# Transposes of quad 4 dealt into batch 0's scores, and four single PSUM banks as two rings of two

## The chip, the cores and the metric

The kernel runs on one core of one Trainium2 chip. The metric is the device time of one execution in microseconds (us), as the median of several runs. A core has a matrix engine (PE), a vector engine (DVE), a scalar engine for activations (ACT), a general engine (POOL) and a queue engine (SP). Each takes its instructions in the order of its own list; they wait for one another through semaphores. Results of the PE land in PSUM, eight banks of 128 x 512 float32, from which DVE or ACT must read them out before the bank can be written anew.

## The reference

Sigmoid attention over 8 batches of 12 heads, followed by a two-layer network with SiLU:

```python
S = q.shape[2]                                     # q, k, v: (8, 12, 448, 64)
scores = np.matmul(q, k.transpose(0, 1, 3, 2)) / np.sqrt(64) - np.log(S)
attn = 1.0 / (1.0 + np.exp(-scores))
attn_out = np.matmul(attn, v)
x = attn_out.transpose(0, 2, 1, 3).reshape(8 * 448, 768)
h = x @ w_in                                       # w_in: (768, 2048)
g = h * (1.0 / (1.0 + np.exp(-h)))
out = g @ w_out                                    # w_out: (2048, 768)
```

Inputs and output are float32; the kernel computes in float16 with float32 sums.

## The kernel before

**Quads and units.** The work of attention is cut into quads: four heads of one batch, so three quads for a batch and 24 in all. Quad g has seven chunks of keys (ch = 0 to 6), and one chunk of one quad is a unit, numbered n = 7g + ch. For a unit, `scores` issues four 64x64 matmuls (L196) into a pair of PSUM banks (`psc`, two buffers of two banks) and one sigmoid on ACT (L207) that writes `attnT`. `values` multiplies the seven chunks with v (L232, four matmuls for a chunk, 28 for a quad) into two single banks `pav`, one for each half of the rows, and DVE copies them to `xT` (L243). `values(g, end)` with end below 7 does the rounds up to end and keeps the two banks for a later call.

**Transposes.** The scores need k and q with the head's dimension on partitions. For quads 0 to 5 the PE transposes them: `pe_transpose` (L145) takes a list of pieces, and for each takes one single bank (`ptrk` or `ptrq`), issues two matmuls for a chunk against an identity (L153), and has DVE, or ACT for two pieces of quad 0 (L143), copy the bank to `kT` or `qT` (L160). `transposes(g, "k")` is two pieces, chunks 0 to 3 and 4 to 6, so 14 matmuls and two copies; both copies must be done before the quad's scores. Later quads are transposed by DMA.

**The network.** `h_unit(b, fc)` is six matmuls of 128x448 (L262) into a single bank `ph`, then a sigmoid on ACT (`tsig`, L274) and a product on DVE that reads the bank (`gTr`, L276). The second layer's products go to single banks too (`po`, L338). All of this is one generator, `stream`, of which `stretch(ns)` issues a portion.

**Single banks.** Four of the eight PSUM banks are one pool, `ps_1`, with four buffers under one tag. `pw` (dummy matmuls of `keep_busy`), `ptr`, `pav`, `ph`, `po` and some scores (`psc1`) all draw from it. A new tile takes a bank that an earlier tile had, and its first matmul waits for that tile's readers.

**Order of batch 0.** The order is written out by hand. After quad 0's transposes a loop issues `scores` for n = 0 to 23, and behind each what the table `behind` (L554) lists for that n: the rest of quad 0's k, dummy matmuls, transposes of quads 1 to 3, rounds of the values of quads 0 to 2, and the first four matmuls of the first two `h_unit`s (`begin`). Then, for n = 24 to 40 in steps of two, `burst(n, 2)` issues the scores of two units and, if a quad has become complete in an earlier burst, its values; transposes of quads 4 and 5 follow at n = 24, 26, 30 and 32; `stretch` follows each burst. The first `stretch` stands before n = 24: it finishes the two units begun and starts the third.

**Loads.** q, k, v and the weights are loaded by POOL's queue in program order (L82, L113, L120), eight in flight. Further loads are issued when a quad's transposes or values are placed (`after_transpose`, `after_values`).

Of the kernel before, what the change touches and what calls it, by code (L numbers as in the profile page):

```python
# [11 lines left out]
F32 = mybir.dt.float32  # L12
# [5 lines left out]
def kernel(  # L18
# [14 lines left out]
    P = 128  # L33
# [18 lines left out]
    p4 = ctx.enter_context(tc.tile_pool(name="p4", bufs=4))  # L52
    p12 = ctx.enter_context(tc.tile_pool(name="p12", bufs=12))
    ps_sc = ctx.enter_context(tc.tile_pool(name="ps_sc", bufs=2, space=bass.MemoryType.PSUM))
    ps_1 = ctx.enter_context(tc.tile_pool(name="ps_1", bufs=4, space=bass.MemoryType.PSUM))
    ctx.enter_context(tc.manual_schedule())

# [7 lines left out]
    def new_flat(name, g):  # L67
        flat[name, g] = (p3 if name == "v" else p4).tile(
            [P, 2, NCH, D], F16, tag=f"{name}f", name=f"{name}f"
        )  # L70

    def rows_in(name, g):
        b, iq = divmod(g, NQ)
        return source[name][b, 4 * iq : 4 * iq + 4].rearrange(
            "(i h) (p c) d -> (h p) i (c d)", h=2, c=NCH
        )

    def load(names, g, c0=0, c1=NCH):
        for name in names:
            if (name, g) not in flat:  # L80
                new_flat(name, g)
            nc.gpsimd.dma_start(  # L82
                flat[name, g][:, :, c0:c1].rearrange("p i c d -> p i (c d)"),
                rows_in(name, g)[:, :, c0 * D : c1 * D],
            )
# [22 lines left out]
    def load_w_in(step):  # L108
        cols = slice(step * DFF // 4, (step + 1) * DFF // 4)
        rows = moe_w_in[:, cols].rearrange("(iq j h d) f -> h j d iq f", j=2, h=2, d=D)  # L110
        for half in range(2):
            for j in range(2):
                nc.gpsimd.dma_start(  # L113
                    w_in_sb[j * D : (j + 1) * D, half * NQ : (half + 1) * NQ, cols], rows[half, j]
                )
# [13 lines left out]
    def new_qkT(g):  # L129
        for name in ("k", "q"):  # L130
            qkT[name, g] = p4.tile([P, NCH, P], F16, tag=f"{name}T", name=f"{name}T")
# [3 lines left out]
    def keep_busy(n):  # L135
        if n == 0:
            return
        pw = ps_1.tile([P, 512], F32, tag="ps1", name="pw")
        for _ in range(n):
            nc.tensor.matmul(pw, dummy[:, :P], dummy, start=True, stop=True)  # L140

# [3 lines left out]
    def pe_transpose(g, pieces=(("k", 0, 4), ("k", 4, NCH), ("q", 0, 4), ("q", 4, NCH))):  # L145
        if ("k", g) not in qkT:
            new_qkT(g)
        for name, c0, c1, *copy in pieces:
            dst = qkT[name, g].rearrange("p c t -> p (c t)")
            ptr = ps_1.tile([P, 512], F32, tag="ps1", name=f"ptr{name}")  # L150
            for c in range(c0, c1):
                for j in range(2):
                    nc.tensor.matmul(  # L153
                        ptr[j * D : (j + 1) * D, (c - c0) * P : (c - c0 + 1) * P],
                        flat[name, g][:, j, c, :],
                        ident,
                        start=True,
                        stop=True,
                    )
            (copy[0] if copy else nc.vector.tensor_copy)(  # L160
                dst[:, c0 * P : c1 * P], ptr[:, : (c1 - c0) * P]
            )
# [14 lines left out]
    def late_sigmoid():  # L177
        while late:
            to, psc = late.pop()
            nc.scalar.activation(to, psc, AF.Sigmoid, bias=bias_s, scale=QKSCALE)  # L180
# [26 lines left out]
            nc.scalar.activation(to, psc, AF.Sigmoid, bias=bias_s, scale=QKSCALE)  # L207

    def single_banks():
        return [ps_1.tile([P, 512], F32, tag="ps1", name="psc1") for _ in range(2)]  # L210

    xT = {}
    ready = set()
# [4 lines left out]
    def values(g, end=NCH):  # L218
        b, iq = divmod(g, NQ)
        if b not in xT:  # L220
            assert b < 2 or b - 2 in h_done
            xT[b] = p2.tile([P, NPAIR, S], F16, tag="xT", name="xT")
        pav, done_rounds = part_of.pop(g, None) or (
            [ps_1.tile([P, 512], F32, tag="ps1", name="pav") for _ in range(2)],
            0,
        )
        for ch in range(done_rounds, end):
            at = attnT.pop((g, ch))
            for half in range(2):
                own = slice(half * HP, (half + 1) * HP)  # L230
                for j in range(2):
                    nc.tensor.matmul(  # L232
                        pav[half][j * D : (j + 1) * D, :S],
                        flat["v", g][own, j, ch, :],
                        at[own, j, :],
                        start=(ch == 0),
                        stop=(ch == NCH - 1),
                    )
        if end < NCH:
            part_of[g] = pav, end  # L240
            return
        for half in range(2):
            nc.vector.tensor_scalar_mul(xT[b][:, half * NQ + iq, :], pav[half][:, :S], SX)  # L243
        if iq == NQ - 1:
            ready.add(b)
# [9 lines left out]
    def h_unit(b, fc):  # L255
        nonlocal hold, weight
        weight = H_WEIGHT if b > 1 else 1.0
        hold = b > 1 and fc >= NFC - 2 or b == 1 and fc == NFC - 1
        ph = ps_1.tile([P, 512], F32, tag="ps1", name="ph")
        for at, cc in enumerate(pairs):  # L260
            assert b in ready or at < 4
            nc.tensor.matmul(  # L262
                ph[:, :S],
                w_in_sb[:, cc, fc * P : (fc + 1) * P],
                xT[b][:, cc, :],
                start=(at == 0),
                stop=(at == NCC - 1),
            )
            if at < NCC - 1:
                yield 189  # L270
        if fc == NFC - 1:
            h_done.add(b)
        tsig = p3.tile([P, S], F16, tag="tsig", name="tsig")
        nc.scalar.activation(tsig, ph[:, :S], AF.Sigmoid, bias=0.0, scale=ISX)  # L274
        late_sigmoid()
        nc.vector.tensor_mul(  # L276
            gTr[:, fc, (b % 2) * S : (b % 2) * S + S], ph[:, :S], tsig
        )
        yield 189
# [39 lines left out]
    def out_set(a1, rows1, a2, rows2, last=False):  # L319
# [13 lines left out]
        left, right, whole = slice(0, NO2), slice(NO2, DMODEL), slice(0, DMODEL)  # L333

        def product(a, w):
            po = ps_1.tile([P, 512], F32, tag="ps1", name="po")
            for fc in range(NHC):
                nc.tensor.matmul(  # L338
                    po[:, :NO2], a[:, fc, :], w[:, fc, :], start=(fc == 0), stop=(fc == NHC - 1)
                )  # L340
                if fc < NHC - 1:
                    yield 163
            return po[:, :NO2]
# [8 lines left out]
        po = yield from product(a1[:, lo], wq[0][0])  # L352
# [5 lines left out]
        po = yield from product(a1[:, hi], wq[1][0])  # L358
# [5 lines left out]
        po = yield from product(sg[2], tw[3])  # L364
        plus(c22, po, m1)
        yield 163
        po = yield from product(sg[1], tw[2])
# [3 lines left out]
        po = yield from product(a2[:, hi], tw[4])  # L371
        plus(c21, po, c22, -ISX)
        yield 163
        po = yield from product(sg[0], tw[1])
# [4 lines left out]
        po = yield from product(sg[3], wq[1][1])  # L379
# [95 lines left out]
    load("v", 1)  # L475
    load("v", 2)
    load("kq", 3)
    load_w_in(0)

    nc.vector.memset(dummy, 0.5)  # L480
    nc.vector.memset(bias_s, NEG_LOG_S)
# [9 lines left out]
    def after_transpose(g):  # L491
        if g == 0:
            load("kq", 4)
            load_w_in(1)
        elif g == 1:
            load("kq", 5)
        elif g == 4:
            load("kq", 8)
# [24 lines left out]
    def values_if_any():  # L523
        if waiting:
            g = waiting.pop(0)
            values(g)
            after_values(g)

    keep_busy(9)
    pe_transpose(  # L530
        0, (("q", 0, SPLIT), ("k", 0, 1, act_copy), ("q", SPLIT, NCH, act_copy), ("k", 1, FIRST))
# [8 lines left out]
    def transposes(g, name):  # L540
        pe_transpose(g, ((name, 0, 4), (name, 4, NCH)))
        if name == "q":
            after_transpose(g)
# [6 lines left out]
    def begin(fc, steps):  # L550
# [3 lines left out]
    behind = {  # L554
        1: ((rest_of_first_k,),),
        2: ((keep_busy, 2),),
        3: ((transposes, 1, "k"),),
        4: ((transposes, 1, "q"),),
        5: ((keep_busy, 2),),
        6: ((keep_busy, 2),),  # L560
        7: ((keep_busy, 2),),
        8: ((transposes, 2, "k"),),
        9: ((transposes, 2, "q"),),
        10: ((rounds, 0, 2),),
        11: ((rounds, 0, 4),),
        12: ((rounds, 0, 7),),
        13: ((transposes, 3, "k"),),
        14: ((transposes, 3, "q"),),
        15: ((rounds, 1, 2),),
        16: ((rounds, 1, 4),),  # L570
        17: ((rounds, 1, 7),),
        18: ((rounds, 2, 2),),
        19: ((rounds, 2, 4),),
        20: ((rounds, 2, 6),),
        21: ((begin, 0, 4),),
        22: ((rounds, 2, 7),),
# [2 lines left out]
    for n in range(NT_B + 3):  # L579
        scores(*units[n])  # L580
        for do, *what in behind.get(n, ()):
            do(*what)

    TILES = {2: 3, 3: 2, 4: 3, 5: 3, 6: 3, 7: 3}
    paces = {1: 1600, 2: 2400, 3: 2500, 4: 3400, 5: 3200, 6: 3000, 7: 2800}
# [11 lines left out]
    stretch(paces[1])  # L597
    for n in range(NT_B + 3, 2 * NT_B, 2):
        burst(n, 2)
        if n in (24, 30):  # L600
            transposes(4 + (n - 24) // 6, "k")
        elif n in (26, 32):
            transposes(4 + (n - 26) // 6, "q")
        stretch(paces[1])
    values_if_any()
    stretch(21500)
    n = 2 * NT_B
# [39 lines left out]
```

## Time and profile before

| what | us |
|---|---|
| median of three runs | 378.68 (378.37 to 378.78) |
| the profiled execution | 379.04 |
| its span, first to last instruction | 377.3 |
| PE busy in the span | 368.2 |
| ACT busy | 242.9 |
| DVE busy | 234.3 |
| POOL busy | 66.3 |

Starts and lengths in the lines below are in us from the first instruction. In the chain of waits a line is a start, a length and what the chain was on; in the timeline a line is a start, the length of a merged stretch, engine, line of the kernel, operation, what it writes and reads, how many instructions were merged, and in brackets the idle time of the engine before it with what ended it. Matmuls overlap in the PE, so a stretch's length reaches past the start of what follows; the next start tells what the stretch took. A digit in the rows of 40 slices is the busy share of that slice in tenths; one slice is 9.4 us.

### The profile page before, as it was taken

How to read it: one execution, taken by the hardware profiler on the slowest of the kernel's cores; microseconds unless marked ns; L12 is line 12 of the kernel's file. 1: busy time of each engine (PE TensorE's matmuls, PEld its weight loads, DVE VectorE, ACT ScalarE, POOL GpSimd, SP SyncE). 2: the span in 40 equal slices, each digit the busy share in tenths (PEclk: the TensorE clock that was granted, in tenths of full speed). 3: DMA queues.
4: the chain of work that ended last, by engine and by line, in shares of the span. 5: the costliest groups of instructions: out<-in, count | busy, mean ns of one | idle time of the engine just before them, and what ended most of it. 6: DMA issues, size and time to landing. Idle time of an engine off the chain costs nothing.

```text
span 377.3 us, 7624 instructions
## 1 busy us (share of the span) xinstructions
PE 368.2 (98%) x3081; PEld 188.7 (50%) x3081; DVE 234.3 (62%) x417; ACT 242.9 (64%) x355; POOL 66.3 (18%) x99
## 2 busy tenths in 40 slices
PE   7899999999999999999999999999999999999995
PEld 2444445555554455455555545544555445555663
DVE  3456646997666566548577557645676457556773
ACT  5998886778767776676556666667866685243000
POOL 8566423052211103102120200000000000000000
PEclk9999999999999999999999999999999999999999
DMA  8999999989999909919599744546062300110333
GB/s 136 199 204 204 204 204 203 178 126 131 228 208 199 119 2 108 180 42 102 75 162 195 100 111 75 40 118 75 0 138 46 85 2 2 51 33 2 82 86 83
DMA packets 65698, 42.79 MB, mean 113 GB/s; under 512 B 36096, under 2 KB 62208, under 8 KB 65664
## 3 DMA queue, kind: packets, MB, share of 16 engines
q0 software_dynamic: 27072, 22.58, 42.3%
q1 hardware_dynamic: 38240, 19.44, 27.3%
q8 instruction: 24, 0.39, 0.4%
q10 hardware_dynamic: 352, 0.30, 0.2%
q14 instruction: 10, 0.08, 0.1%
HBM read 45.61 MB, written 11.01 MB: 150 GB/s over the span
## 4 chain that ended last, share of the span: by engine, by line
PE 90%; ACT 5%; DMA 2%; issue 1%; POOL 1%; DVE 0%; POOLq 0%; ACTq 0%
PE ph L262 39%; PE po L338 34%; PE psc L196 9%; PE pav L232 8%; ACT attnT L207 4%; DMA qf<-in_q_dram 2%; POOL kf L82 1%; PE ptrq L153 0%; PE ptrk L153 0%; ACT attnT L180 0%; DVE gTr L276 0%; DVE osb L346 0%; ACT kept L412 0%; ACT m L353 0%; ACT tsig L274 0%
## 5 line engine op out<-in xcount | busy, mean ns | idle before, releaser
L207 ACT ACTIVATE attnT<-psc,bias_s 128x896 f16<-128x896 f32 (+1 forms) x168 | 138.2, 896 | 46.1 <-PE psc L196 45.9
L262 PE MATMUL ph<-xT,w_in_sb 128*128 128x448 f16 x768 | 151.2, 353 | 0.0
L276 DVE TENSOR_TENSOR gTr<-ph,tsig 128x448 f16<-128x448 f32 x128 | 78.2, 622 | 69.0 <-ACT tsig L274 68.4
L262 PEld LDWEIGHTS <-w_in_sb 128*128 128x128 f16 x768 | 72.8, 98 | 73.6 <-issue 8.2
L274 ACT ACTIVATE tsig<-ph 128x448 f16<-128x448 f32 x128 | 68.2, 548 | 49.3 <-PE ph L262 48.9
L338 PEld LDWEIGHTS <-S 128*128 128x128 f16 x448 | 42.3, 98 | 33.5 <-issue 6.8
L346 DVE SCALAR_TENSOR_TENSOR osb<-po,osb 128x384 f32<-128x384 f32 x70 | 37.6, 553 | 22.2 <-PE po L338 22.0
L196 PE MATMUL psc<-qT,kT 64*64 64x448 f16 x672 | 48.4, 360 | 1.7 <-ACT qT L143 0.6
L243 DVE TENSOR_SCALAR xT<-pav 128x448 f16<-128x448 f32 x48 | 27.7, 619 | 31.0 <-PE pav L232 31.0
L82 POOL DMA_DIRECT2D vf<-in_v_dram x24 | 17.2, 719 | 163.0 <-PE pav L232 138.8
L338 PE MATMUL po<-T,S 128*128 128x384 f16 x224 | 40.6, 327 | 0.0
L338 PEld LDWEIGHTS <-gTr 128*128 128x128 f16 x304 | 28.7, 98 | 23.5 <-issue 5.4
L338 PE MATMUL po<-w_out_sb,S 128*128 128x384 f16 x224 | 39.9, 326 | 0.0
L232 PE MATMUL pav<-attnT,vf 64*64 64x448 f16 x672 | 38.4, 350 | 0.7 <-DVE gTr L276 0.4
L338 PE MATMUL po<-w_out_sb,gTr 128*128 128x384 f16 x192 | 34.9, 327 | 0.0
L196 PEld LDWEIGHTS <-kT 64*64 64x64 f16 x672 | 16.1, 105 | 29.6 <-issue 25.4
L346 DVE SCALAR_TENSOR_TENSOR osb<-po,m 128x384 f32<-128x384 f32 x42 | 23.2, 552 | 6.3 <-PE po L338 5.2
L232 PEld LDWEIGHTS <-vf 64*64 64x64 f16 x672 | 20.5, 107 | 12.7 <-issue 2.7
L180 ACT ACTIVATE attnT<-psc,bias_s 128x896 f16<-128x896 f32 x26 | 26.5, 1021 | 0.0
L353 ACT ACTIVATE m<-po 128x384 f32<-128x384 f32 x14 | 6.9, 494 | 23.7 <-PE po L338 23.7
L338 PE MATMUL po<-T,gTr 128*128 128x384 f16 x112 | 21.4, 326 | 0.0
L82 POOL DMA_DIRECT2D kf<-in_k_dram x25 | 18.1, 725 | 17.6 <-DVE kr L168 11.1
(43 smaller groups left out, 154.4 us busy)
## 6 DMA issues: line engine op xcount, KB each, us to landing
out_dram<-osb SPq DMA_DIRECT2D x54, 192.0 KB, 3.3
vf<-in_v_dram POOLq DMA_DIRECT2D x24, 224.0 KB, 5.6
kf<-in_k_dram POOLq DMA_DIRECT2D x23, 224.0 KB, 6.8
qf<-in_q_dram POOLq DMA_DIRECT2D x23, 224.0 KB, 7.5
w_in_sb<-in_moe_w_in_dram POOLq DMA_DIRECT2D x16, 192.0 KB, 7.9
w_out_sb<-in_moe_w_out_dram POOLq DMA_DIRECT2D x4, 768.0 KB, 14.9
kT<-kr SPq DMA_TRANSPOSE x18, 6.5
qT<-qr SPq DMA_TRANSPOSE x18, 6.3
```

The costliest lines, as they stand in the source:

```text
L82: nc.gpsimd.dma_start(flat[name, g][:, :, c0:c1].rearrange("p i c d -> p i (c d)"), rows_in(name, g)[:, :, c0 * D : c1 * D],)
L180: nc.scalar.activation(to, psc, AF.Sigmoid, bias=bias_s, scale=QKSCALE)
L196: nc.tensor.matmul(banks[j][own, :S], qkT["k", g][rows, ch, own], qkT["q", g][rows, :, own], start=True, stop=True,)
L207: nc.scalar.activation(to, psc, AF.Sigmoid, bias=bias_s, scale=QKSCALE)
L232: nc.tensor.matmul(pav[half][j * D : (j + 1) * D, :S], flat["v", g][own, j, ch, :], at[own, j, :], start=(ch == 0), stop=(ch == NCH - 1),)
L243: nc.vector.tensor_scalar_mul(xT[b][:, half * NQ + iq, :], pav[half][:, :S], SX)
L262: nc.tensor.matmul(ph[:, :S], w_in_sb[:, cc, fc * P : (fc + 1) * P], xT[b][:, cc, :], start=(at == 0), stop=(at == NCC - 1),)
L274: nc.scalar.activation(tsig, ph[:, :S], AF.Sigmoid, bias=0.0, scale=ISX)
L276: nc.vector.tensor_mul(gTr[:, fc, (b % 2) * S : (b % 2) * S + S], ph[:, :S], tsig)
L338: nc.tensor.matmul(po[:, :NO2], a[:, fc, :], w[:, fc, :], start=(fc == 0), stop=(fc == NHC - 1))
L346: nc.vector.scalar_tensor_tensor(out=o, in0=po, scalar=sign, in1=x, op0=ALU.mult, op1=ALU.add)
L353: nc.scalar.activation(m1, po, AF.Copy, scale=ISX)
```

## The change

Three things are altered.

The pool `ps_1` gets two tags of two banks each, `ps0` and `ps1`. A helper `bank` chooses: with `fixed` set to 0, as it is from the first dummy matmuls to the end of the loop over n = 0 to 23, all tiles but `pav` are in `ps0` and `pav` is in `ps1`; after that the two alternate tile by tile.

The table `behind` is dealt anew. Quad 1's transposes stand at n = 4 and 5 instead of 3 and 4, quad 4's at n = 16 and 18 instead of behind the bursts at 24 and 26; the rounds of values of quads 0 and 1 are at other n; five dummy matmuls stand in the loop instead of eight. Quad 5's transposes are behind the bursts at 28 and 30 instead of 30 and 32.

The first quarter of `w_in` is loaded behind quad 4's k and q instead of ahead of them. Since `after_transpose(4)` is now called in the loop, quad 8's k and q are loaded ahead of v of quad 5 and the second half of `w_out`.

```diff
-    ps_1 = ctx.enter_context(tc.tile_pool(name="ps_1", bufs=4, space=bass.MemoryType.PSUM))
+    ps_1 = ctx.enter_context(tc.tile_pool(name="ps_1", bufs=2, space=bass.MemoryType.PSUM))
     ctx.enter_context(tc.manual_schedule())
+
+    side = 0
+    fixed = None
+
+    def bank(name, own=None):
+
+        nonlocal side
+        if own is None:
+            own = fixed
+        if own is None:
+            own = side
+            side = 1 - side
+        return ps_1.tile([P, 512], F32, tag=f"ps{own}", name=name)
...
-        pw = ps_1.tile([P, 512], F32, tag="ps1", name="pw")
+        pw = bank("pw")
...
-            ptr = ps_1.tile([P, 512], F32, tag="ps1", name=f"ptr{name}")
+            ptr = bank(f"ptr{name}")
...
-        return [ps_1.tile([P, 512], F32, tag="ps1", name="psc1") for _ in range(2)]
+        return [bank("psc1") for _ in range(2)]
...
-            [ps_1.tile([P, 512], F32, tag="ps1", name="pav") for _ in range(2)],
+            [bank("pav", None if fixed is None else 1 - fixed) for _ in range(2)],
...
-        ph = ps_1.tile([P, 512], F32, tag="ps1", name="ph")
+        ph = bank("ph")
...
-            po = ps_1.tile([P, 512], F32, tag="ps1", name="po")
+            po = bank("po")
...
-    load_w_in(0)
...
         if g == 0:
             load("kq", 4)
+            load_w_in(0)
             load_w_in(1)
...
+    fixed = 0
     keep_busy(9)
...
-        3: ((transposes, 1, "k"),),
-        4: ((transposes, 1, "q"),),
-        5: ((keep_busy, 2),),
-        6: ((keep_busy, 2),),
-        7: ((keep_busy, 2),),
+        3: ((keep_busy, 2),),
+        4: ((transposes, 1, "k"),),
+        5: ((transposes, 1, "q"),),
+        6: ((rounds, 0, 2),),
+        7: ((rounds, 0, 4),),
         8: ((transposes, 2, "k"),),
         9: ((transposes, 2, "q"),),
-        10: ((rounds, 0, 2),),
-        11: ((rounds, 0, 4),),
-        12: ((rounds, 0, 7),),
+        10: ((rounds, 0, 7),),
+        11: ((keep_busy, 1),),
+        12: ((rounds, 1, 2),),
         13: ((transposes, 3, "k"),),
         14: ((transposes, 3, "q"),),
-        15: ((rounds, 1, 2),),
-        16: ((rounds, 1, 4),),
+        15: ((rounds, 1, 5),),
+        16: ((transposes, 4, "k"),),
         17: ((rounds, 1, 7),),
-        18: ((rounds, 2, 2),),
-        19: ((rounds, 2, 4),),
+        18: ((transposes, 4, "q"),),
+        19: ((rounds, 2, 3),),
         20: ((rounds, 2, 6),),
...
+    fixed = None
...
         burst(n, 2)
-        if n in (24, 30):
-            transposes(4 + (n - 24) // 6, "k")
-        elif n in (26, 32):
-            transposes(4 + (n - 26) // 6, "q")
+        if n in (28, 30):
+            transposes(5, "k" if n == 28 else "q")
         stretch(paces[1])
```

## The prediction

> **What bounds the kernel now.** I read the summary of engines and the 40 slices first, then the chain of work that ended last (whole, and cut to the first 60 us), then five-us windows, then the timeline around the places that the change touches.
>
> ```profile
> PE 368.2 (98%) x3081; PEld 188.7 (50%) x3081; DVE 234.3 (62%) x417; ACT 242.9 (64%) x355; POOL 66.3 (18%) x99
> ACT  5998886778767776676556666667866685243000
> ...
> PE 90%; ACT 5%; DMA 2%; issue 1%; POOL 1%; DVE 0%; POOLq 0%; ACTq 0%
> ```
>
> The PE is busy 368.2 of 377.3 us and holds 90% of the chain; the 5% of ACT and 2% of DMA lie early, where the ACT row shows 8s and 9s.
>
> ```profile
> 4.03 7.24 DMA qf<-in_q_dram
> ...
> 12.26 5.99 ACT attnT L207 x7
> ...
> 28.07 2.68 PE ph L262 x13
> ```
>
> So there are three stages. Until 11.27 us the chain is the load of quad 1's q. From 12.26 it is batch 0's sigmoids on ACT (scores units n = 0 to 23, starts 0.889 us apart), the PE only filling time. From 28 us it is the PE without a break: what is added to or taken from the PE's order there, waits included, moves the end one for one. Each sigmoid end lets the PE begin the scores two units on (psc has two buffers).
>
> ```profile
> 10.71 1.02 ACT L207 ACTIVATE attnT<-psc,bias_s 128x896 f16<-128x896 f32 x1
> 11.31 0.58 PE L153 MATMUL ptrq<-ident,qf 128*64 128x128 f16 x14 [0.94 <-DMA qf<-in_q_dram]
> 11.83 0.38 PE L196 MATMUL psc<-qT,kT 64*64 64x448 f16 x4
> 12.26 1.90 ACT L207 ACTIVATE attnT<-psc,bias_s 128x896 f16<-128x896 f32 x2 [0.53 <-PE psc L196]
> ```
>
> Here q of quad 1 is late; the scores behind it in the PE's order are late too, and sigmoid 5 starts at 12.26 instead of 10.71 + 0.89 = 11.60: ACT loses 0.66 us.
>
> **The change, part by part.** Three dummy matmuls go (8 to 5 among the scores); they lay in PE time that ACT covers, price nothing. The 28 transposes of quad 4 move from the PE stage into the ACT stage. Banks: in the loop over n everything but pav now shares two banks, pav has the other two. Which instruction then waits for which reader is in the list of waits of the changed program; I priced each new one with rows of before. Releases reach the PE about 0.05 us after the reader's end (sigmoid end 9.04, next scores 9.09).
>
> 1. *Start.* The second q piece of quad 0 now waits for ACT's copy of the first k piece.
>
> ```profile
> 5.71 0.33 PE L153 MATMUL ptrq<-ident,qf 128*64 128x128 f16 x6
> ...
> 5.92 0.28 ACT L143 ACTIVATE kT<-ptrk 128x128 f16<-128x128 f32 x1 [1.51 <-PE ptrk L153]
> ```
>
> It starts at 6.20 + 0.05 = 6.25 instead of 5.71, and through the qT copy the first sigmoid is 0.54 late (7.67). Without the wait for q at n=4 (moved a slot on) ACT then runs on: sigmoid 5 at 11.60 + 0.54 = 12.14, 0.12 before the old time. So the slot's gain of 0.66 is nearly spent.
>
> 2. *Quad 1.* q follows k one slot later in the same two banks. Scores 4 start when sigmoid 2 ends (8.93 + 0.54 + 1.00, + 0.06 = 10.53); k's transposes 0.31 later at 10.84. From 14.69 to 16.30, a k transpose's start to the end of its second copy is 1.61, so the second q piece starts at 10.84 + 1.61 + 0.05 = 12.50, scores 6 some 0.30 later at 12.80, sigmoid 6 0.44 after that (11.83 to 12.26): 13.24 against 13.17 before. Running total +0.07.
>
> 3. *Quads 2 and 3* stand k, q in neighbouring slots as before, but q now waits for k's copies.
>
> ```profile
> 14.69 0.58 PE L153 MATMUL ptrk<-ident,kf 128*64 128x128 f16 x14
> 15.15 1.15 DVE L160 CAST kT<-ptrk 128x512 f16<-128x512 f32 x2 [2.22 <-PE ptrk L153]
> ...
> 15.52 0.58 PE L153 MATMUL ptrq<-ident,qf 128*64 128x128 f16 x14
> ```
>
> Scores follow 1.91 (1.61 + 0.05 + 0.25 for six transposes) after k's start instead of 1.34 (16.03), 0.57 later. Scores 10 started 0.69 before their sigmoid (16.72) and need 0.44, so 0.25 is slack: at most 0.31 lost, and nothing if the scores ahead go earlier. I take 0.25 for each pair, 0.50 for two.
>
> 4. *Quad 4 and values.* k at n=16, q at n=18: the slot between covers the copies. Quad 2's rounds at n=19 now meet quad 1's xT copies of DVE (1.16 the pair) in pav's two banks: 0 to 0.24, taken 0.10. DMA order: k and q of quad 4 go ahead of the first quarter of w_in on POOL's queue. In before that quarter and quad 4 land in one run that ends at 25.73, and the total is the same, so w_in's quarter lands at about 25.7 and quad 4 two transfers of 1.1 us after quad 3's q (19.62), k at 20.7 and q near 22; their first users come at 26.4 (ph) or later, and at 21.7 and 23.5 (scores 16 and 18 of before at 21.40 and 23.20, plus 0.3): covered. Quad 8's k and q go ahead of v of quad 5 and w_out's second half, 2 x 1.1 us, which have some 4 us of cover (v lands 50.27, its values run at 56.20). Price nothing. Items 1 to 4: sigmoid 23 is 0.67 late (bounds -0.12, the pairs in the slack, to 0.93, all of it).
>
> 5. *First unit after the scores.* The third ph unit (five matmuls inside the row at 28.00, the first at 29.64) took a pav bank, long free. In the changed program it waits for the gTr product of the first ph unit, which stands behind ACT's whole queue of sigmoids.
>
> ```profile
> 28.66 1.00 ACT L207 ACTIVATE attnT<-psc,bias_s 128x896 f16<-128x896 f32 x1
> 29.45 1.30 PE L262 MATMUL ph<-xT,w_in_sb 128*128 128x448 f16 x6
> 29.55 0.98 ACT L274 ACTIVATE tsig<-ph 128x448 f16<-128x448 f32 x2
> 30.12 1.16 DVE L276 TENSOR_TENSOR gTr<-ph,tsig 128x448 f16<-128x448 f32 x2 [1.10 <-ACT tsig L274]
> ```
>
> That product ends at 30.75 (first of the two, 0.62 long), so the PE resumes at 30.80 instead of 29.64: +1.16 on top of the 0.67. Behind it in the PE's order stand scores 24 and 25, so ACT starves too.
>
> 6. *Transposes gone from there.* -0.51 (31.18 to 31.69) and -0.70 (33.81 to 34.51). ACT limits how much is cashed: a burst without transposes is 0.5 + 1.6 to 1.8 of PE, but 2 x 0.889 + 1.4 x 0.423 = 2.37 of ACT, some 0.17 more in each of two. -1.21 + 0.35 = -0.86 (bounds -1.21 to -0.5).
>
> 7. *Quad 5 a slot earlier.* k's transposes now stand at n=28, right behind quad 3's values; the second piece waits in the list of waits for the xT copy of the second pav.
>
> ```profile
> 38.15 1.69 PE L262 MATMUL ph<-xT,w_in_sb 128*128 128x448 f16 x8
> 38.25 1.16 DVE L243 TENSOR_SCALAR xT<-pav 128x448 f16<-128x448 f32 x2 [1.38 <-PE pav L232]
> ```
>
> Piece one takes the place of the ph at 38.15 and 0.21; piece two could start at 38.36 but waits until 39.41 + 0.05: +1.10 (bounds 0.9 to 1.3). From some 60 us on the two programs wait alike.
>
> Sum: 0.67 + 1.16 - 0.86 + 1.10 = +2.07 (bounds 0.73 to 2.89). The span of 377.3 becomes 379.4; 1.7 us lie around it (profiled execution 379.04), and that execution is 0.36 over the median of 378.68. So 378.68 + 2.07 = 380.7 us.
>
> **Rivals.** *Faster:* the ACT run ends early enough that the gTr release of item 5 is out of the way. It decides if that release comes 1.16 us sooner; the only thing to give is the 0.66 at n=5, against the 0.54 of the start. Were the bank waits all hidden, -0.12 - 0.86 gives 377.7. Against it: the waits stand in the program and their readers' times in the rows. *The stalls pay back:* while the PE waits at 39 ACT catches up, and the hole of 0.41 at 48.70 (pav waiting for gTr) closes, with the 0.35 of item 6: 380.0. For it: ACT is what is late there. *Loads late:* quad 4's k has about one us of cover; a load a us later than its cover at each of n=16 and n=21, less the 0.25 slack, is +1.5 at most, 382.2. Against it: landings there came 1.1 us apart without fail. *Clock:* more PE holes could lower the granted clock; it was 1.00 in every window, the one with 0.94 idle included, and a five-us window at half speed would cost at most 5, 385.7. The Trainium skill (TensorE: Matmul & The Clock Gate, "A second HAM failure mode: psum-queue depth-cycling") warns that short PE idles from cycling through PSUM banks make the clock swing; by its window of about 3.4 us an estimate is +1.7 for one fall. This trace has such idles and no fall.
>
> **How the numbers follow.** The forecast 0.72, its own range 379.4 to 381.6; stalls paid back 0.14; loads late 0.05; clock 0.02; faster 0.07. Range 379.3 to 381.7: it leaves the faster case, most of the late loads and the clock out, with the tails under 0.2. About 0.2%, 0.76 us, is what a measurement can tell from no change. The lower tail of the forecast and part of the pay-back and of the faster case fall within it: 0.07. Slower 0.88, faster 0.05.
>
> **What would show it.** First sigmoid near 7.7, sigmoid 23 near 29.3, PE idle over 1 us before an L275 ph (L262 before) near 31 with gTr as releaser, and before a ptrk near 40 with xT as releaser; no transposes between 32 and 36. I am wrong if the third ph starts before 30.5, if ptrk's second piece finds its bank free, or if the PE idles on a DMA between 20 and 27.

## The result and the profile after

| | before | after |
|---|---|---|
| median of the runs | 378.73 (378.37 to 378.83, 6 runs) | 381.38 (380.99 to 381.72, 6 runs) |
| ratio, 95% interval | | 1.0071 (1.0058 to 1.0084) |
| the profiled execution | 379.04 | 381.53 |
| its span | 377.3 | 379.8 |

The changed kernel is slower by 2.65 us in the medians and by 2.49 us in the two profiled executions. From the page of the changed kernel, the summary of engines and the shares of the chain that ended last:

```profile
span 379.8 us, 7616 instructions
...
PE 368.9 (97%) x3078; PEld 189.4 (50%) x3078; DVE 234.5 (62%) x417; ACT 243.0 (64%) x355; POOL 66.0 (17%) x99
...
PE 91%; ACT 4%; DVE 2%; issue 1%; ACTq 0%
```

The engines have nearly the same work as before (the PE 368.9 us with three matmuls fewer against 368.2, DVE 234.5 against 234.3); most of what the span grew by is waiting. DMA's 2% of the chain are gone, and DVE, which had 0%, has 2%: copies out of PSUM are now waited for. The list of waits of the changed kernel, from 5 to 45 us (engine and line that waited, what for; us in total, times, longest):

```profile
PE ph L275 <- DVE gTr L289: 1.0, 1, 1.0
PE ptrk L166 <- DVE xT L256: 0.9, 1, 0.9
PE ptrq L166 <- DVE kT L173: 0.8, 3, 0.3
...
PE ptrq L166 <- ACT kT L156: 0.4, 1, 0.4
```

These are four kinds of wait for single banks: the third ph behind the first gTr, quad 5's k behind the values' xT, q behind k in three quads, and q behind k at the start. The timeline of the changed kernel shows each at its place:

```profile
6.20 0.28 ACT L156 ACTIVATE kT<-ptrk 128x128 f16<-128x128 f32 x1 [1.63 <-PE ptrk L166]
...
6.52 0.36 PE L166 MATMUL ptrq<-ident,qf 128*64 128x128 f16 x6 [0.37 <-ACT kT L156]
...
30.99 1.16 DVE L289 TENSOR_TENSOR gTr<-ph,tsig 128x448 f16<-128x448 f32 x2 [1.10 <-ACT tsig L287]
31.66 1.11 PE L275 MATMUL ph<-xT,w_in_sb 128*128 128x448 f16 x5 [1.00 <-DVE gTr L289]
...
39.56 1.16 DVE L256 TENSOR_SCALAR xT<-pav 128x448 f16<-128x448 f32 x2 [0.70 <-PE pav L245]
...
40.77 0.36 PE L166 MATMUL ptrk<-ident,kf 128*64 128x128 f16 x6 [0.90 <-DVE xT L256]
```

Each PE row starts about 0.05 us after the end of the reader that it waited for: 6.20 + 0.28 = 6.48 to 6.52, the first gTr at 30.99 + some 0.62 to 31.66, the second xT at 39.56 + 1.16 = 40.72 to 40.77.

Cutting the span at the starts of sigmoids (n is the unit) shows where the time went. Every number in the rows of before and after is a difference of two starts in one trace, save the first column, which is a start, and the last, which runs to the end of the last matmul:

| stretch, us | first sigmoid | 0 to 23 | 23 to 24 | 24 to 28 | 28 to 30 | 30 to 34 | 34 to 40 | 40 to the last matmul |
|---|---|---|---|---|---|---|---|---|
| before | 7.13 | 21.52 | 2.52 | 5.58 | 3.56 | 5.35 | 9.19 | 318.25 |
| after | 7.89 | 21.63 | 3.68 | 4.84 | 5.18 | 4.93 | 9.20 | 318.25 |
| difference | +0.76 | +0.11 | +1.16 | -0.74 | +1.62 | -0.42 | +0.01 | 0 |

The sum is +2.50. All of it arises by the start of sigmoid 40; behind it nothing is paid back: 318.25 us are the same to the hundredth. The third ph costs 1.16. Moving quad 4's transposes gives back 0.74. Quad 5's costs 1.62 - 0.42 = 1.20.

### The profile page after: what moved, and what is told of

Same layout as the page of the kernel before. It is cut to its first block, busy times and chain, and to the rows that moved or that the text cites. A ratio compares the mean times of both kernels' runs of the same rounds, so it can differ in the third digit from the quotient of the medians.

```text
span 379.8 us, 7616 instructions
## 1 busy us (share of the span) xinstructions
PE 368.9 (97%) x3078; PEld 189.4 (50%) x3078; DVE 234.5 (62%) x417; ACT 243.0 (64%) x355; POOL 66.0 (17%) x99
## 4 chain that ended last, share of the span: by engine, by line
PE 91%; ACT 4%; DVE 2%; issue 1%; ACTq 0%
PE ph L275 37%; PE po L351 34%; PE psc L209 10%; PE pav L245 8%; ACT attnT L220 3%; PE pw L153 1%; PE ptrq L166 1%; DVE kT L173 1%; DVE xT L256 0%; ACT tsig L287 0%; PE ptrk L166 0%; DVE gTr L289 0%; DVE qT L173 0%; ACT attnT L193 0%; DVE osb L359 0%
```

## The experiments

Each edit is against the changed kernel unless another is named; none leaves out or changes any part of what is computed.

### Quad 5's transposes back behind the bursts at 30 and 32 (q5_back)

```diff
-        if n in (28, 30):
-            transposes(5, "k" if n == 28 else "q")
+        if n in (30, 32):
+            transposes(5, "k" if n == 30 else "q")
```

> The changed kernel with quad 5's transposes put back behind the bursts at n = 30 and 32. Theory (each late wait is paid once, in full): the second k piece of quad 5 no longer stands right behind quad 3's values, its wait of 0.93 us for the second xT copy goes and with it the late restart, 1.0 to 1.1 less than the changed kernel's 381.38: about 380.3. The idle PE before the third ph unit, 1 us, stays. Rival (ACT is what is late there, the stall only stands in for another): 0.3 less at most, 381.1 or more, with a new PE wait on ACT or on a gTr between 38 and 50 us.

Measured: 380.36 (379.46 to 381.66), ratio to before 1.0051 (1.0036 to 1.0066). In the trace sigmoids 0 to 28 start as in the changed kernel, 28 to 30 takes 3.58 instead of 5.18 and 30 to 34 again 5.35; the last matmul ends 1.20 earlier. The wait of quad 5's k for a bank of the values is worth that much.

### The third ph on a bank of pav (third_ph)

```diff
     fixed = None
+    side = 1
```

The alternation begins with the other ring, so the third ph finds a bank that has long been free.

> The changed kernel with the alternation after the scores begun at the other ring, so that the third ph unit takes a pav bank and waits for no gTr. Theory: its 1.16 us go, about 380.2; PE runs from the second ph unit into the third, which starts near 30.5, and scores 24 follow near 31.6 instead of 32.77. Rival (the ACT run sets the pace, the bank only names it): scores 24 wait for ACT anyway and under 0.4 is won, 381.0 or more.

Measured: 381.04 (379.76 to 382.51), ratio 1.0066 (1.0045 to 1.0088), a wide spread. The trace decides: 23 to 24 takes 2.52, as in before, instead of 3.68, and 28 to 30 keeps its 5.18. So the wait is that of this bank, 1.16 us, and the two late waits are independent. The six runs fall into two groups, three from 379.76 to 380.39, around the expected 380.2, and three from 381.68 to 382.51; the median lies between them. The profiled execution is the highest, and what it has too much lies at the start of the kernel; that is taken up in the last section.

### Both late waits out (both)

```diff
     fixed = None
+    side = 1
...
-        if n in (28, 30):
-            transposes(5, "k" if n == 28 else "q")
+        if n in (30, 32):
+            transposes(5, "k" if n == 30 else "q")
```

> Both edits at once. Theory: the two waits are separate and add, 381.38 - 1.1 - 1.16 = 379.1, with 0.3 to 0.5 left over the kernel before (378.73): the 0.87 by which sigmoid 23 is late, less the part of the moved transposes that ACT lets through. Rival (they hide one another, or ACT holds): 380.0 or more.

Measured: 378.95 (378.46 to 379.25, 11 runs), ratio 1.0012 (1.0003 to 1.0021). In its list of waits, same columns, same stretch, the PE has no wait for gTr or xT left, only those of the start and of the score stage:

```profile
PE ptrq L166 <- DVE kT L173: 0.8, 3, 0.3
PE psc L209 <- ACT attnT L220: 0.7, 2, 0.5
PE psc L209 <- ACT qT L156: 0.4, 1, 0.4
PE ptrq L166 <- ACT kT L156: 0.4, 1, 0.4
```

And in five-us windows the PE, busy 4.00 and 4.23 of 5 in the changed kernel (first fence, from 30 and from 40; columns: PE, PEld, DVE, ACT, POOL busy, granted clock, DMA share, GB/s), is without idle time (second fence):

```profile
30.00:35.00 5.00, 4.00 (x28) 1.59 (x28) 1.16 (x2) 3.19 (x6) 2.89 (x6) 1.00 1.24 204
...
40.00:45.00 5.00, 4.23 (x43) 2.16 (x43) 4.04 (x8) 2.76 (x4) 2.17 (x3) 1.00 1.31 204
```

```profile
30.00:35.00 5.00, 5.00 (x36) 2.11 (x36) 1.75 (x4) 4.35 (x8) 2.69 (x5) 1.00 1.24 204
...
40.00:45.00 5.00, 5.00 (x60) 2.54 (x61) 3.56 (x7) 4.63 (x7) 1.93 (x3) 1.00 1.31 204
```

Two small edits take back 2.2 us (0.0071 - 0.0012 of 378.7). The rest of the loss is in the start and the score stage, which still have the rings.

### The new deal with one ring of four banks (one_pool)

```diff
-    ps_1 = ctx.enter_context(tc.tile_pool(name="ps_1", bufs=2, space=bass.MemoryType.PSUM))
+    ps_1 = ctx.enter_context(tc.tile_pool(name="ps_1", bufs=4, space=bass.MemoryType.PSUM))
...
-        return ps_1.tile([P, 512], F32, tag=f"ps{own}", name=name)
+        return ps_1.tile([P, 512], F32, tag="ps1", name=name)
```

> The new deal of the table and of the loads, all as in the changed kernel, but the four single banks one ring again. Theory (the rings lose the time, not the deal): the list of waits has no wait of quad 0's q piece for a copy and none of the third ph unit for gTr; the k piece of quad 5 still stands behind the values but waits for the first xT copy instead of the second, 0.5 earlier. So -1.16, -0.3 to -0.6 of the start and -0.5: 379.1 to 379.4. Rival (the deal loses it, the k-q pairs and values wait for DVE whatever the banks): 380.8 or more.

Measured: 378.75 (378.23 to 379.14, 11 runs), ratio 1.0005 (0.9996 to 1.0013). So the deal as a whole, without the rings, cannot be told from before, and lies below what was expected (379.1 to 379.4). Waits of the PE, same columns, same stretch:

```profile
PE ptrq L166 <- DVE kT L173: 0.4, 2, 0.2
PE ptrk L166 <- DVE xT L256: 0.4, 1, 0.4
```

Quad 5's k still waits for xT behind the values, only for the first copy instead of the second: 28 to 30 takes 4.65, between 3.56 and 5.18. Four banks in a ring soften this wait; they do not remove it.

### The rings with the old deal (old_deal_rings)

The table `behind` and the places of quads 4 and 5 are those of before; the rings and the changed order of loads stay.

> The reverse of the one ring: the old table and the old places of quads 4 and 5, with the two rings of two (the weights' and quad 4's loads stay in the changed order, as does quad 5's in the loads). Theory (the rings lose the time): 0.54 or more at the start, 0.2 to 0.45 for each of three k-q pairs in neighbouring slots, 1.16 for the third ph unit, nothing given back: 1.9 to 3 over the kernel before, 380.4 to 381.5. Rival (the deal loses it): 379.0 or less.

Measured: 382.1 (381.48 to 382.29), ratio 1.0089 (1.0075 to 1.0103). This is above what was expected; the reason is in the waits of the PE, from 5 to 34 us:

```profile
PE ptrq L166 <- DVE kT L173: 1.1, 3, 0.6
PE ph L275 <- DVE gTr L289: 1.0, 1, 1.0
...
PE pav L245 <- DVE xT L256: 0.5, 2, 0.4
```

With the old deal, rounds of the next quad come upon pav's two banks while DVE still copies them (0.5 us), and the pairs of k and q wait longer (1.1 against 0.8): sigmoids 0 to 23 take 22.62 instead of 21.63. The new deal takes back 1.0 us of what the rings cost in this stage. It was not measured which of the new deal's places does it.

### Rings only after quad 0's transposes (both_start), from the kernel with both late waits out

```diff
-    fixed = 0
     keep_busy(9)
...
+    fixed = 0
+
     def rest_of_first_k():
```

> Both late waits out (as before), and the two rings begin only after quad 0's first transposes, so that its second q piece waits for no copy. Theory: the first sigmoid comes 0.54 earlier than with the rings (near 7.3), the ACT run with it, and the end 0.3 to 0.5 earlier than 378.95: 378.5. Rival (quad 1's q lands late and takes back what the start gives): within 0.15 of 378.95.

Measured: 378.67 (378.07 to 379.05, 11 runs), ratio 1.0000 (0.9991 to 1.0009). The wait of q for ACT's kT copy is gone from its list of waits, the first sigmoid starts at 7.50 instead of 7.89 (in the kernel with both late waits out), and 0 to 23 keeps its 21.63.

### Quad 4's transposes back behind the bursts (both_q4_back), from the same kernel

```diff
-        16: ((transposes, 4, "k"),),
+        16: ((keep_busy, 1),),
...
-        18: ((transposes, 4, "q"),),
+        18: ((keep_busy, 1),),
...
-        if n in (28, 30):
-            transposes(5, "k" if n == 28 else "q")
+        if n in (24, 30):
+            transposes(4 + (n - 24) // 6, "k")
+        elif n in (26, 32):
+            transposes(4 + (n - 26) // 6, "q")
```

> Both late waits out, and quad 4's transposes back behind the bursts at n = 24 and 26, with one dummy matmul in each of their two slots among the scores. It prices the move alone. Theory: 1.0 us of PE come back into the stage that the PE bounds, less the 0.3 that ACT did not let through: 0.5 to 0.9 over 378.95, about 379.6. Rival (ACT bounds those bursts, the move is worth nothing): 379.1 or less.

Measured: 379.76 (379.46 to 381.99, 8 runs), ratio 1.0038 (1.0022 to 1.0054), against 1.0012 with quad 4 in the score stage. In the trace 24 to 28 takes 5.58 again instead of 4.84, and 0 to 23 is 21.63 with the transposes there or without. So the move that gives the change its name is worth 0.74 us and costs the score stage nothing. One of the eight runs, 381.99, lies 2.1 above the others; the last section comes back to it.

### One ring and quad 5 left in its place (one_pool_q5)

The edits of one_pool and q5_back together.

> The new deal with one ring of four, and quad 5's transposes back at n = 30 and 32. Theory: the last new wait, quad 5's k behind quad 3's values (0.4 at the first piece and more behind it), goes: 0.5 to 0.7 under the 378.75 of the one ring, 378.1, and so faster than the kernel before by 0.3 to 0.5. Rival: the hole of 0.41 before the pav at 48 grows by what is won, 378.6 or more.

Measured: 378.14 (377.66 to 378.5, 11 runs), ratio 0.9986 (0.9978 to 0.9995): faster than both kernels, by 0.5 us against before.

### The same with quad 2's q a slot later (one_ring_q2_apart)

```diff
-        9: ((transposes, 2, "q"),),
-        10: ((rounds, 0, 7),),
-        11: ((keep_busy, 1),),
+        9: ((keep_busy, 1),),
+        10: ((transposes, 2, "q"),),
+        11: ((rounds, 0, 7),),
```

> The new deal with one ring of four banks and quad 5's transposes left at n = 30 and 32 (as in the earlier run of these three, 378.14), and quad 2's q moved from n = 9 to n = 10, with the dummy matmul between k and q and rounds of quad 0 to 7 at n = 11. Theory: a pair of transposes in neighbouring slots costs the sigmoids up to 0.25 us even with four banks, because 28 transposes stand ahead of one score; with the slot between them sigmoid 23 comes 0.1 to 0.3 earlier than in that run (28.655) and the time is 377.8 to 378.1. Rival: with four banks the pair lies in the slack of the psc buffers, sigmoid 23 and the time are those of that run within 0.1.

Measured: 378.2 (377.36 to 378.45, 12 runs), ratio 0.9989 (0.9981 to 0.9998). In the trace sigmoids 0 to 23 take 21.16 instead of 21.30, so the pair in neighbouring slots does cost 0.14; the medians are too coarse to show it, and the time is the same as that of the kernel above.

### The kernel before with quad 1 a slot later (before_slot)

```diff
-        3: ((transposes, 1, "k"),),
-        4: ((transposes, 1, "q"),),
-        5: ((keep_busy, 2),),
+        3: ((keep_busy, 2),),
+        4: ((transposes, 1, "k"),),
+        5: ((transposes, 1, "q"),),
```

> The kernel before with one part of the change alone: quad 1's transposes at n = 4 and 5, the two dummy matmuls of n = 5 at n = 3. Theory: the wait for quad 1's q (0.94 us of PE idle ahead of the last scores before sigmoid 5) no longer stands in front of scores 5, so the sigmoids run on from n = 4 without the gap and sigmoid 5 starts near 11.6 instead of 12.26; of these 0.66 us the later quads give some back, since quad 1's scores stand a slot nearer to its transposes. Sigmoid 23 between 28.0 and 28.5 (28.66 before), the time between 378.1 and 378.4. Rival: the wait moves to scores 6 with its whole length and nothing is gained: sigmoid 23 at 28.6 to 28.7, the time 378.7 within 0.2.

Measured: 378.71 (378.13 to 378.97, 11 runs), ratio 1.0005 (0.9997 to 1.0014): no gain. Yet in its trace the sigmoids run without the gap. The chain of waits, from 0 to 60 us:

```profile
7.47 10.53 ACT attnT L207 x12
```

Twelve sigmoids stand in one piece where the chain of before broke off for the load of q until 11.27, and 0 to 23 takes 20.93 instead of 21.52. The theory had the mechanism and missed the time; the next run says why.

### The kernel before, profiled once more (before_again)

> The kernel before, unchanged, profiled once more. Theory: the late q of quad 1 (landed 11.27, 0.94 us of PE idle, 0.66 us of ACT) belonged to that one profiled execution; in the twelve profiles of the other kernels, whose first loads are issued at the same instants, it landed at 9.71 to 10.40. So here it lands in that band, sigmoid 5 follows the first sigmoid by 4.4 to 4.6 us (5.13 in the first profile) and sigmoid 23 follows it by 20.9 to 21.0 (21.52). Rival: the order of the kernel before makes q late, since its loads behind the first seven differ: it lands after 11, sigmoid 23 follows the first by 21.5.

Measured: 378.77 (378.21 to 378.88, 8 runs), profiled execution 378.48. Its timeline at the same place as the second extract of the prediction:

```profile
8.95 4.60 ACT L207 ACTIVATE attnT<-psc,bias_s 128x896 f16<-128x896 f32 x5
...
10.33 0.42 PEld L153 LDWEIGHTS <-qf 128*64 128x64 f16 x14 [0.20 <-DMA qf<-in_q_dram]
10.33 0.58 PE L153 MATMUL ptrq<-ident,qf 128*64 128x128 f16 x14
10.84 0.19 PEld L196 LDWEIGHTS <-kT 64*64 64x64 f16 x4
10.91 0.38 PE L196 MATMUL psc<-qT,kT 64*64 64x448 f16 x4
```

Quad 1's q landed at 10.16 here, against 11.27; its transposes start at 10.33 instead of 11.31, the scores behind them at 10.91 instead of 11.83, and the sigmoids run on: 0 to 23 takes 20.90, all other stretches are those of the first profile to 0.01. In all 14 profiles but the first, q landed between 9.71 and 10.40. The gap of 0.66 us in the first profile was a late load of that one execution, not a property of the kernel; why that load was late is open.

### The third ph on a pav bank, rings after quad 0's transposes (third_ph_start)

The edits of third_ph and of both_start's `fixed = 0`, with quad 5 where the changed kernel has it.

> The changed kernel with the third ph unit on a pav bank, and the two rings beginning only after quad 0's first transposes, so that these find free banks; quad 5's transposes stay behind quad 3's values. Theory: the late third ph is worth 1.16 and the start some 0.3 to 0.4, so 381.4 - 1.5 = 379.9 (379.6 to 380.2), the stall of about 1.1 us at n = 30 is kept, and with no bank waits at the start no run shows the clock of TensorE held back (mean granted clock 0.997 or more in every run). Rival on the clock: where it is held back does not hang on the bank waits of the start, and some runs of this kernel spread upward by 1.5 to 2.5 us with a mean clock of 0.993, as two of the six of the kernel with the third ph moved did.

Measured: 379.91 (379.44 to 380.16), ratio 1.0040 (1.0027 to 1.0053). The mean clock is 0.999 or more in all five runs; that alone would not decide, since it reads 0.998 in the disturbed execution of third_ph too, but none of the five times stands out upward. Stretch 28 to 30 is 5.18 as expected, 0 to 23 21.63, 23 to 24 2.52.

### All of them in one table

The stretches repeat from kernel to kernel so exactly that they can be added up. In each row: differences to before_again's trace (20.90, 2.52, 5.58, and 3.56 + 5.35 = 8.91 for 28 to 34). One execution's first sigmoid scatters by some 0.6 us with the instant at which the PE reaches full speed (last section), so for it means are taken: 7.84 in the five undisturbed profiles with rings from the first dummy (7.66 to 7.89), 7.24 in the eight without (6.88 to 7.50), so +0.60 or 0. Of these 0.60 some 0.1 to 0.2 is chance: between traces with nearly the same instant of full speed the rings cost 0.39 to 0.53. "Measured" is the ratio less one times 378.7, with its interval.

| kernel | start | 0 to 23 | 23 to 24 | 24 to 28 | 28 to 34 | sum | measured |
|---|---|---|---|---|---|---|---|
| the changed kernel | 0.60 | 0.73 | 1.16 | -0.74 | 1.20 | 2.95 | 2.69 (2.20 to 3.18) |
| q5_back | 0.60 | 0.73 | 1.15 | -0.74 | 0.02 | 1.76 | 1.93 (1.36 to 2.50) |
| third_ph (0 to 23 from both) | 0.60 | 0.73 | 0 | -0.74 | 1.20 | 1.79 | 2.50 (1.70 to 3.33) |
| both | 0.60 | 0.73 | 0 | -0.74 | 0.02 | 0.61 | 0.45 (0.11 to 0.80) |
| both_start | 0 | 0.73 | 0 | -0.74 | 0.02 | 0.01 | 0.00 (-0.34 to 0.34) |
| both_q4_back | 0.60 | 0.73 | 0 | 0 | -0.01 | 1.32 | 1.44 (0.83 to 2.04) |
| one_pool | 0 | 0.40 | 0 | -0.74 | 0.67 | 0.33 | 0.19 (-0.15 to 0.49) |
| one_pool_q5 | 0 | 0.40 | 0 | -0.74 | 0.02 | -0.32 | -0.53 (-0.83 to -0.19) |
| one_ring_q2_apart | 0 | 0.26 | 0 | -0.74 | 0.02 | -0.46 | -0.42 (-0.72 to -0.08) |
| third_ph_start | 0 | 0.73 | 0 | -0.74 | 1.20 | 1.19 | 1.51 (1.02 to 2.01) |
| old_deal_rings | 0.60 | 1.72 | 1.15 | 0 | -0.01 | 3.46 | 3.37 (2.84 to 3.90) |
| before_slot | 0 | 0.03 | 0 | 0 | 0 | 0.03 | 0.19 (-0.11 to 0.53) |

All twelve sums lie in the measured intervals, though the traces are single executions and the medians are over others. With 0.45 for 0.60 at the start eleven still do; third_ph's 1.64 is then 0.06 short of its interval, which its three long runs raise. With the first profile of before as the base (21.52 instead of 20.90) every sum would be 0.62 lower, and ten of the twelve would fall out of their interval.

The columns also part the deal from the rings. The deal alone, with one ring (one_pool), costs 0.40 in 0 to 23, gives 0.74 back in 24 to 28 and costs 0.67 behind quad 3's values. The rings add 0.33 in 0 to 23, 1.16 at the third ph, 0.53 behind the values and 0.39 to 0.53 at the start. The changed order of loads stands in all the kernels of the table but before_slot, so it was not taken out alone and is part of the deal here; in none of the changed traces does the PE wait for a load before 40 us.

## Why the prediction was right, and where a term was not

The time came out 0.7 us above the predicted 380.7, on the side and by the mechanism forecast: waits for banks of the two rings.

*Item 1, the start.* The wait is there, q behind ACT's kT copy; priced at 0.54, it is 0.39 to 0.53 at the same instant of full speed (0.60 between the means). Of the 0.76 by which the two first traces differ, some 0.34 is that instant and not the change: 5.38 us in before, 6.25 in after, and before_slot, without rings and with 6.29, has its first sigmoid at 7.47. What failed is the other half of that item, "ACT loses 0.66 us" to the late q, which the slot was credited with saving: before_again shows that the kernel normally loses nothing there, and before_slot that the slot saves nothing. The prediction noted that the profiled execution was 0.36 above the median and carried the whole sum over to the median all the same; that 0.36 points to this wait (before_again, without it, came out at 378.48), and the saving should have been left out with it. Without it the same working gives 2.07 + 0.66 = 2.73 and 381.4. That this meets 381.38 so closely is partly luck: among the other terms the start was put too high, by up to 0.15, and item 4 by at least 0.10, the pairs 0.13, item 6 0.12 and item 7 0.10 too low.

*Item 2, quad 1.* Sigmoid 6 was put at 13.24 with the first at 7.67, 5.57 after it; it came 5.56 after it. In before_again it comes 5.35 after.

*Item 3, the pairs.* Against before_again, counted from the first sigmoid, the delay grows by 0.20 across quad 2's pair (n = 6 to 10) and by 0.43 across quad 3's (14 to 15), each priced at 0.25. The second has a wait that was not priced, two units ahead of it in the PE's order. The timeline of the changed kernel:

```profile
17.76 1.16 DVE L256 TENSOR_SCALAR xT<-pav 128x448 f16<-128x448 f32 x2
...
18.97 0.14 PEld L245 LDWEIGHTS <-vf 64*64 64x64 f16 x5 [0.42 <-issue]
...
19.66 0.58 PE L166 MATMUL ptrk<-ident,kf 128*64 128x128 f16 x14
...
20.86 0.82 PE L166 MATMUL ptrq<-ident,qf 128*64 128x128 f16 x14 [0.31 <-DVE kT L173]
21.61 0.38 PE L209 MATMUL psc<-qT,kT 64*64 64x448 f16 x4
21.82 0.55 PE L245 MATMUL pav<-attnT,vf 64*64 64x448 f16 x8
22.11 1.01 ACT L220 ACTIVATE attnT<-psc,bias_s 128x896 f16<-128x896 f32 x1 [0.29 <-PE psc L209]
```

Quad 1's first rounds (n = 12) need a pav bank that DVE copies until 17.76 + 1.16 = 18.92, and the PE goes on at 18.97. That quad 3's k, at 19.66, is late by this wait is read from the order, not from a run in which it alone was taken out.

*Item 4.* Priced at 0.10; from n = 15 to 23 the changed kernel takes 7.41, before_again 7.54, so it cost nothing. Quad 4's loads had landed before their users and the PE has no wait for a DMA there: no late load came in.

*Item 5, the third ph.* Priced at 1.16, measured 1.16, and removed by its own edit.

*Items 6 and 7.* Quad 4's transposes were to give 0.86 and gave 0.74. Quad 5's wait was priced at 1.10: the PE stands from 39.45 + 0.21 to 40.77, 1.11. But the net of moving quad 5 is 1.20, since of the 0.51 that its transposes free after n = 30 only 0.42 is cashed; the price of a move is what it costs at the new place less what the old place really gives back.

*The rivals.* The stalls were not paid back: the hole in which pav waits for gTr, 0.41 at 48.70 in before, is 0.44 long, at 51.21. The clock did not fall in the idle stretches at 31 and 40: the granted clock is 1.00 in these windows, and the five matmuls of the ph after the wait take 1.11, as such rows do elsewhere (1.12 at 33.21). The warning of the Trainium skill (TensorE: Matmul & The Clock Gate, "A second HAM failure mode: psum-queue depth-cycling") is thus not borne out there by this trace. The faster case needed the bank waits hidden; with one ring and quad 5 in its place they nearly are, and the deal is then the faster one by 0.0014 (0.0005 to 0.0022).

## What to carry over

Splitting a ring of PSUM banks in two does not only change how many banks there are: it changes whose reader a tile waits for, and a reader that stands behind another engine's queue (here gTr behind ACT's sigmoids, 1.16 us; xT behind a whole quad of values, 1.11 us) stops the PE at the one place where nothing covers it. List for each tile the reader that it inherits, and move work towards idle time only together with that list. And before a wait in a profile is counted as something to win, look at a second profile: a DMA that landed 0.9 us later than in any other profiled execution made a gap of 0.66 us that no change could win back.

## What was not expected of the hardware

The PE runs at half speed at first: in the trace of before the dummy matmuls of the start begin 0.43 us apart, the two at n = 2 0.23 apart. Its full speed sets in at another instant in each execution, and the later it sets in, the later comes the first sigmoid, up to 7.89 with the rings (in us, by the clock records of 13 traces; the dummies start at 1.46 in all of them):

| before quad 0's transposes | full speed from | first sigmoid |
|---|---|---|
| no rings | 4.84, 5.25, 5.38, 5.49, 5.91, 6.04, 6.29, 6.53 | 6.88, 7.09, 7.13, 7.16, 7.36, 7.36, 7.47, 7.50 |
| rings | 5.53, 6.03, 6.25, 6.40, 6.42 | 7.66, 7.89, 7.89, 7.89, 7.89 |

At half speed the first eight transposes are a stretch of 0.64 us (both_start), at full speed of 0.41 (before). The PE waits for no load there in any of these traces.

In third_ph's profiled execution full speed set in only at 14.22. Its timeline:

```profile
11.47 1.04 PE L153 MATMUL pw<-dummy 128*128 128x512 f16 x2
...
12.96 0.96 PE L166 MATMUL ptrk<-ident,kf 128*64 128x128 f16 x14
13.85 0.54 PE L209 MATMUL psc<-qT,kT 64*64 64x448 f16 x4
```

and the same instructions of the kernel with both late waits out, whose order is the same up to here:

```profile
10.16 0.61 PE L153 MATMUL pw<-dummy 128*128 128x512 f16 x2
10.75 0.38 PE L209 MATMUL psc<-qT,kT 64*64 64x448 f16 x4
11.06 0.58 PE L166 MATMUL ptrk<-ident,kf 128*64 128x128 f16 x14
```

Two dummies take 1.04 instead of 0.61 and 14 transposes 0.96 instead of 0.58, while the column of the granted clock reads 1.00 in these windows: ahead of the first record of the clock that column says nothing, the durations do. The sigmoids starve: 0 to 23 takes 23.38 instead of 21.63, and that execution took 382.51. The mean clock of the run does not show it: it reads 0.998 there, as in many undisturbed runs. The time does. Of the 42 runs of kernels that have the rings from the first dummy on, five lie 1.2 to 2.1 us above the highest other run of their kernel: this one, two more of third_ph (381.71 and 381.68) and one of q5_back (381.66), all three with a mean clock of 0.993, and one of both_q4_back (381.99, 0.999). Of the 61 runs of the other edited kernels none lies more than 0.4 above the median of its kernel, and third_ph_start had none in five. Only one of the five was profiled, so a late full speed is shown for that one alone. That the short idle times at the start are the cause is likely by this and not shown, since the other 37 runs with the same idle times show nothing of it. The Trainium skill (TensorE: Matmul & The Clock Gate, "What's actually happening") says that full speed comes after a busy window of about 3.4 us whose place is free-running, so that the instant varies by 0.5 us either way from run to run. The lengths of the stretches at full speed in the 14 traces agree with such a window: they are 365.22, 368.64 or 372.05 us, in steps of 3.41. The instants from 4.84 to 6.53 spread somewhat wider, 0.85 either way, and 14.22 lies far outside.
